# Block two's transposes by VectorE squares and DRAM, and Fourier tables as one row per product

## The chip, the cores and the metric

The kernel runs on one core of one Trainium2 chip. The metric is the device time of one execution in microseconds (us). Engines are named as the profile names them: PE is TensorE (PEld its weight loads), DVE is VectorE, ACT is ScalarE, POOL is GpSimd, SP is SyncE, which issues most DMAs.

## The reference

Three stages run one after the other on 4 batches of 768 tokens with 320 features.

- Attention: a recurrence over 768 steps with a 40 x 40 state for each of 4 batches and 8 heads.
- Block one: the real part of a two-dimensional Fourier transform (over tokens and over features) is added to x; the sum u is normalised over features, and `u + relu(un @ w_ch1) @ w_ch2` is the result (320 to 1280 to 320).
- Block two: `u = x + (relu(xt @ w_tok1) @ w_tok2)` over tokens (768 to 256 to 768), and then `u + relu(u @ w_ch1) @ w_ch2` over features (320 to 1536 to 320).

## The kernel before

Every operation of the program is first written into a plan (class `Plan`, L64) with its engine, an estimated cost, what it reads and writes, and a stage name. `emit` (L104) then simulates the engines and writes the instructions in the order in which the simulation starts them. Of the operations that are ready on an engine it takes the one with the smallest latest start, which is the length of the path behind it times a factor, plus an offset for each stage from the table `OFF` (L637). So one program order per engine comes out, and the engines keep to it. While the simulation sees PE with nothing to do it may put in small matmuls on an identity matrix (`warm`, L50), which compute nothing that is used.

Numbers are kept in two parts, a high one and a low one, each of a type that PE multiplies at its fast rate; a product is high x high, high x low and low x high, summed in PSUM.

Block one, for each batch b:

- `fft(b)` (L828) folds the tokens and the features, splits the result into `Xh` and `Xl`, and multiplies with the table `T1`, separately for even and odd frequencies (`par`). For each of 4 blocks of features, 3 chunks k of tokens and 2 parities it issues three matmuls into columns of one PSUM tile `psA` of 386 columns: Xh with the table's high part, Xh with its low part, Xl with its high part (L860). Three tiles (m = 0, 1, 2) hold both parities. Then ACT copies each parity of each tile into the high part `A` (L867) and DVE writes PSUM minus that into the low part (L868, L869).
- `fft2(b)` (L874) multiplies `A` with the table `T2` over features (`mix`), adds the result to X and takes the statistics.
- `norm` (L903) writes the normalised rows `un`; `turn` (L919) transposes three tiles of 128 tokens by 320 features on PE (nine 128 x 128 transposes into three PSUM tiles `trp`), ACT copies each into the high part `th`, DVE subtracts for the low part `tl` (L927 to L929). A turn serves one half (384 tokens) of a batch.
- `ch(b, half)` (L932) is the pair of products: for each of 10 columns of weights (12 in block two) one `hps` group of 8 matmuls with 384 columns (L953), ACT relu to `hh`, DVE to `hl` (L955, L956), and one `acc` group of 9 matmuls with 320 columns (L943).

Block two runs `tok(b)` (L1004, matmuls `tps`), `tok2(b)` (L1021, matmuls `t2ps`, whose results DVE adds to X), then `twice` (L911), which duplicates the last 64 features into `un`, then `turn` and `ch`. The order in which the plan is written is turn, turn, tok of the next batch, ch of half 0, tok2 of the next batch, ch of half 1; the planner moves them. The first half's output `ou` is written to DRAM by SP when its `ch` is done.

In the background, until 620 us, the weights of `ch` and of block two are decoded from their 64-bit form (`job`, L807: four DVE operations, one of ACT, two of POOL, written to DRAM by SP), and POOL's queue loads them back.

The last step of attention and `fft(0)` use the attention's PSUM banks: `fft(0)` takes three of bank group 'c' (`PA`, L1064). In later batches `fft` takes three of group 'ps', which has three buffers.

Of the kernel before, what the change touches and what calls it, by code (L numbers as in the profile page):

```python
# [636 lines left out]
OFF={'chain': 300.8, 'dec2': 5758.7, 'decay': -751.1, 'decode': 395.0, 'fft': -5021.4, 'fft2': -6464.4, 'inv': -1932.1, 'kbts': 226.7, 'kg': -6093.6,  # L637
     'load': -7697.1, 'load2': -587.1, 'load3': 1109.2, 'loada': 4793.9, 'merge': 1886.3, 'mlp': -1698.4, 'out_tile': 4045.5, 'outp': -1277.8,
     'pad': -9598.4, 'pts': -229.1, 'tok': -12470.6, 'tok2': -645.7, 'wdec': -467.6, ('chain', 0): -4282.3, ('chain', 1): -2552.8,
     ('chain', 10): 45.9, ('chain', 11): -8803.9, ('chain', 2): -3582.8, ('chain', 3): 7517.1, ('chain', 4): -1342.6, ('chain', 5): 1812.8,  # L640
     ('chain', 6): -2540.2, ('chain', 7): -577.2, ('chain', 8): 1284.2, ('chain', 9): -4815.7, ('dec2', 0): 2647.0, ('decay', 0): 1051.3,
     ('decay', 1): -1211.8, ('decay', 10): 2428.7, ('decay', 11): 6696.4, ('decay', 2): 7776.8, ('decay', 3): 2789.5, ('decay', 4): 838.9,
     ('decay', 5): -5123.2, ('decay', 6): -648.2, ('decay', 7): -4184.7, ('decay', 8): -115.8, ('decay', 9): 739.3, ('decode', 0): 4394.9,
     ('fft', 0): 1400.8, ('fft', 1): -1517.7, ('fft', 2): 5142.9, ('fft', 3): -772.4, ('fft2', 0): -5713.8, ('fft2', 1): 3968.9, ('fft2', 2): -531.5,
     ('fft2', 3): 3324.0, ('inv', 0): -6627.6, ('inv', 1): -5380.2, ('inv', 2): -2561.0, ('inv', 3): -2007.0, ('inv', 4): -7054.0, ('inv', 5): 772.7,
     ('kbts', 0): 1581.6, ('kbts', 1): 449.0, ('kbts', 10): 7708.3, ('kbts', 11): 4043.7, ('kbts', 2): -1443.5, ('kbts', 3): -321.0,
     ('kbts', 4): 5122.3, ('kbts', 5): -4668.8, ('kbts', 6): 2466.5, ('kbts', 7): -6673.4, ('kbts', 8): -3755.9, ('kbts', 9): -6836.2,
     ('kg', 0): -308.8, ('kg', 1): 2831.3, ('kg', 10): -5700.1, ('kg', 11): -4561.7, ('kg', 2): 1180.2, ('kg', 3): -2794.7, ('kg', 4): -1608.2,
     ('kg', 5): 2804.0, ('kg', 6): 3809.8, ('kg', 7): 991.9, ('kg', 8): -2008.2, ('kg', 9): 473.4, ('load', 0): 487.0, ('load', 1): -244.0,
     ('load', 10): 7910.1, ('load', 11): -2865.2, ('load', 2): -5618.2, ('load', 3): 6666.7, ('load', 4): -4962.2, ('load', 5): -6389.3,  # L650
     ('load', 6): -8728.7, ('load', 7): 2517.8, ('load', 8): -1405.1, ('load', 9): -4750.5, ('load2', 0): -4261.4, ('load2', 1): -2916.3,
# [4 lines left out]
     ('loada', 10): 2332.4, ('loada', 11): 1588.0, ('loada', 2): 15487.7, ('loada', 3): 344.7, ('loada', 4): -5744.5, ('loada', 5): 8816.6,  # L656
     ('loada', 6): 1439.9, ('loada', 7): -398.8, ('loada', 8): -3423.9, ('loada', 9): 7911.3, ('merge', 0): -6399.2, ('merge', 1): 4559.0,
     ('merge', 10): -10316.3, ('merge', 11): 790.3, ('merge', 2): 4278.3, ('merge', 3): 8872.4, ('merge', 4): -4569.1, ('merge', 5): 3968.6,
     ('merge', 6): 3218.1, ('merge', 7): 9397.1, ('merge', 8): -1894.3, ('merge', 9): 5033.2, ('mlp', 0): 6893.6, ('mlp', 1): 1432.8,
     ('mlp', 2): 2520.1, ('mlp', 3): 2527.4, ('out_tile', None): 7714.2, ('outp', 0): 1563.4, ('outp', 1): -4676.1, ('outp', 10): -1619.6,  # L660
     ('outp', 11): 896.2, ('outp', 2): -3595.4, ('outp', 3): 2664.9, ('outp', 4): 3205.8, ('outp', 5): 3534.9, ('outp', 6): 1010.5,
     ('outp', 7): -6340.7, ('outp', 8): 3125.1, ('outp', 9): 6287.3, ('pad', 0): -609.1, ('pts', 0): 3845.3, ('pts', 1): -329.9, ('pts', 10): 2473.5,
     ('pts', 11): 3044.7, ('pts', 2): 3317.6, ('pts', 3): -5427.0, ('pts', 4): -2906.4, ('pts', 5): -795.8, ('pts', 6): 4682.1, ('pts', 7): 1469.9,
# [49 lines left out]
class Mlp:  # L713


    def __init__(s,tc,at,M1,T2d,w,out,dr,NB=4):
# [111 lines left out]
    def fft(s,b):  # L828
# [7 lines left out]
        for par in range(2):
# [15 lines left out]
            c0,cn=(0,194) if par==0 else (194,192)  # L852
            for m,blocks in enumerate((((0,0),),((128,2),),((256,0),(384,2)))):
                for k0,k1 in G:
                    rk=[(v,o,x) for o in ((0,),(128,),(256,417,320,481))[m] for v in ('Xh','Xl') for x in (0,2) if k0<=x<k1]
                    def f(m=m,blocks=blocks,c0=c0,cn=cn,k0=k0,k1=k1):
                        ps=pst(hs[m])
# [3 lines left out]
                    s.pe((.33,.33,.66)[m]*(k1-k0),f,rk+[('T1',k) for k in range(k0,k1)],[('psA',hs[m][0],par),('psb',hs[m][0])]+[('A',a) for a in ((0,1),(2,3),(4,))[m]],alloc=hs[m][0] if par==0 and k0==0 else None,cols=(582,582,1164)[m]*(k1-k0))  # L861
        for m in range(3):
            ka=[('A',a) for a in ((0,1),(2,3),(4,4))[m]]
            for par,(c0,cn) in enumerate(((0,193),(194,192))):
                kp=('psA',hs[m][0],par)
                ev=lambda a,r=slice(0,128),par=par: t["A"][a][r,par:385:2]
                s.act(cn,lambda m=m,c0=c0,cn=cn,ev=ev: nc.scalar.activation(out=ev(2*m),in_=pst(hs[m])[:,c0:c0+cn],func=AF.Copy),[kp,'mid'],[ka[0]],free=[hs[m][0]])  # L867
                if m<2: f=lambda m=m,c0=c0,cn=cn,ev=ev: nc.vector.tensor_tensor(out=ev(2*m+1),in0=pst(hs[m])[:,c0:c0+cn],in1=ev(2*m).bitcast(F32),op=ALU.subtract)  # L868
                else: f=lambda m=m,c0=c0,cn=cn,ev=ev: nc.vector.tensor_tensor(out=ev(4,slice(64,128)),in0=pst(hs[m])[64:,c0:c0+cn],in1=ev(4,slice(64,128)).bitcast(F32),op=ALU.subtract)  # L869
                s.dve(.27,f,[kp,ka[0]],[ka[1]],free=[hs[m][0]])  # L870
# [254 lines left out]
```

## Time and profile before

| | |
|---|---|
| median of 3 runs | 1012.12 us (1011.55 to 1014.07) |
| the profiled execution, its time | 1013.38 us |
| the profiled execution, its span | 1011.3 us, mean granted clock 0.968 |
| PE busy | 954.5 us (94%) |
| PE weight loads busy | 910.6 us (90%) |
| DVE busy | 618.9 us (61%) |
| ACT busy | 440.2 us (44%) |
| POOL busy | 276.4 us (27%) |

The span counts from the first to the last instruction of the profile; the execution's own time is 2.1 us more. Matmuls are pipelined: the time between the starts of two matmuls is what one costs, and it is shorter than the duration that its row shows.

### The profile page before, as it was taken

Reading aid. Unit: us, or ns where it says so; the run is one execution under the profiler, and the core shown is the slowest. Engines: PE = TensorE matmul, PEld = TensorE weight load, DVE = VectorE, ACT = ScalarE, POOL = GpSimd, SP = SyncE. Lnnn points to the kernel's source line nnn. Section 1 sums busy time; section 2 is a strip of 40 time slices with the busy share of each in tenths; the row PEclk is TensorE's granted clock in tenths of the full one; section 3 lists DMA queues with packets and bytes.
Section 4 is the critical chain, followed back from the end, with each engine's and each line's share of the span. In section 5 each row is a group of like instructions: output and inputs, shape, how many; then the busy total and the mean of one; then the engine's idle time right before and its main releaser. Section 6 shows DMA issues by size and latency. Waiting matters only on the chain.

```text
span 1011.3 us, 23650 instructions
## 1 busy us (share of the span) xinstructions
PE 954.5 (94%) x9707; PEld 910.6 (90%) x9707; DVE 618.9 (61%) x1359; ACT 440.2 (44%) x910; POOL 276.4 (27%) x372
## 2 busy tenths in 40 slices
PE   7559999999999998899999999999999999999998
PEld 6548788888888888889999999999999999999998
DVE  8799397978959248998688866325242332323232
ACT  5266778789787663424322341223222222121221
POOL 8133544454653514233444434000000000000000
PEclk9787999999999879999999999999999999999999
DMA  9996878899885967254545446700000000000000
GB/s 212 199 190 129 186 178 177 190 199 216 193 196 150 270 159 278 66 179 135 171 160 162 145 145 219 292 1 1 2 20 1 20 21 1 20 20 1 20 20 21
DMA packets 140719, 125.47 MB, mean 124 GB/s; under 512 B 100867, under 2 KB 118275, under 8 KB 140483
## 3 DMA queue, kind: packets, MB, share of 16 engines
q1 hardware_dynamic: 135811, 100.29, 39.7%
q0 software_dynamic: 4800, 23.67, 6.8%
q8 instruction: 76, 1.25, 0.5%
q14 instruction: 32, 0.26, 0.1%
HBM read 85.40 MB, written 33.75 MB: 118 GB/s over the span
## 4 chain that ended last, share of the span: by engine, by line
PE 54%; DVE 4%; DMA 0%; issue 0%; ACT 0%; DVEq 0%
PE hps L953 23%; PE acc L943 22%; PE t2ps L1030 2%; PE tps L1017 2%; PE mix L887 2%; PE trp L924 1%; PE psA L860 1%; DVE un L908 0%; DVE mdt L820 0%; DVE Xl L848 0%; DVE mda L817 0%; DMA mdraw<-in_moe_w_ch_dram 0%; DVE un L909 0%; DVE A L868 0%; DVE hl L956 0%
## 5 line engine op out<-in xcount | busy, mean ns | idle before, releaser
L956 DVE SCALAR_TENSOR_TENSOR hl<-hps,hh 128x384 fp32r<-128x384 f32 x176 | 98.0, 557 | 250.6 <-ACT hh L955 250.1
L955 ACT ACTIVATE hh<-hps 128x384 fp32r<-128x384 f32 x176 | 86.3, 491 | 339.9 <-PE hps L953 338.8
L953 PE MATMUL hps<-th,v 128*128 128x384 f32 x576 | 142.4, 337 | 0.0
L943 PE MATMUL acc<-v,hh 128*128 128x320 f32 x576 | 129.1, 311 | 0.0
L953 PE MATMUL hps<-th,W 128*128 128x384 f32 x480 | 120.3, 339 | 2.6 <-DVE hl L956 2.6
L943 PE MATMUL acc<-W,hh 128*128 128x320 f32 x480 | 108.5, 312 | 0.0
L953 PEld LDWEIGHTS hps<-th,v 128*128 128x128 f32 x576 | 103.7, 188 | 0.0
L943 PEld LDWEIGHTS acc<-v,hh 128*128 128x128 f32 x576 | 97.5, 188 | 0.0
L953 PEld LDWEIGHTS hps<-th,W 128*128 128x128 f32 x480 | 86.8, 188 | 3.2 <-DVE hl L956 3.0
L943 PE MATMUL acc<-v,hl 128*128 128x320 f32 x288 | 89.0, 309 | 0.0
L821 POOL TENSOR_TENSOR mda<-mda,mdh 128x320 f32<-128x320 f32 (+2 forms) x44 | 46.8, 1063 | 131.1 <-DVE mdt L819 53.7
L943 PEld LDWEIGHTS acc<-W,hh 128*128 128x128 f32 x480 | 82.3, 190 | 0.0
L329 POOL TENSOR_SCALAR_AFFINE_SELECT RT<-RT 64x384 f32<-64x384 f32 x72 | 56.3, 804 | 78.6 <-ACT RT L238 74.9
L943 PE MATMUL acc<-W,hl 128*128 128x320 f32 x240 | 74.6, 311 | 0.0
L319 PE MATMUL kg<-am,bt 120*128 120x192 f32 x242 | 53.1, 364 | 18.3 <-ACT am L238 16.0
L953 PE MATMUL hps<-tl,v 128*128 128x384 f32 x192 | 64.6, 337 | 0.0
L319 PEld LDWEIGHTS kg<-am,bt 120*128 120x128 f32 x242 | 42.9, 207 | 22.3 <-ACT am L238 16.8
L519 POOL TENSOR_SCALAR_AFFINE_SELECT sc<-sc 64x384 f32<-64x384 f32 (+1 forms) x72 | 40.8, 567 | 72.2 <-ACT sc L238 69.7
L509 PE MATMUL sc<-rm,VZd 120*128 120x192 f32 x264 | 56.7, 349 | 3.1 <-DMA VZd<-in_vR_dram 2.0
L52 PE MATMUL warm<-ident 128*128 128x128 f32 x332 | 51.5, 304 | 5.1 <-DVE A L868 3.1
L943 PEld LDWEIGHTS acc<-v,hl 128*128 128x128 f32 x288 | 54.1, 188 | 0.0
L953 PE MATMUL hps<-tl,W 128*128 128x384 f32 x160 | 53.9, 337 | 0.0
(171 smaller groups left out, 2046.8 us busy)
## 6 DMA issues: line engine op xcount, KB each, us to landing
bt<-in_bkR_dram SPq DMA_DIRECT2D x12, 660.0 KB
mdraw<-in_moe_w_ch_dram SPq DMA_DIRECT2D x22, 320.0 KB
wS<-in_wR_dram SPq DMA_DIRECT2D x12, 335.2 KB
a<-in_aR_dram SPq DMA_DIRECT2D x12, 335.2 KB
RT<-a SPq DMA_DIRECT2D x36, 111.7 KB
LT<-in_vT_dram SPq DMA_DIRECT2D x12, 330.0 KB
VZt<-in_vT_dram SPq DMA_DIRECT2D x12, 330.0 KB
VZd<-in_vR_dram SPq DMA_DIRECT2D x12, 330.0 KB
```

The lines of the kernel that those rows point to most:

```text
L52: for x in range(m): nc.tensor.matmul(t[:,128*(x%4):128*(x%4)+128],lhsT=ident,rhs=ident,start=True,stop=True)
L319: nc.tensor.matmul(ps[:,192*x:192*x+192],lhsT=bt[:,g+x].rearrange("p v t -> p (v t)"),rhs=am[:,:,g+x],start=True,stop=True)
L329: nc.gpsimd.affine_select(out=kv,in_=kv,pattern=[[0,3*m],[1,L]],compare_op=ALU.is_gt,fill=0.0,base=0,channel_multiplier=-1)
L509: for x,g in enumerate(gs): nc.tensor.matmul(ps[:,192*x:192*x+192],lhsT=VZd[:,g].rearrange("p v t -> p (v t)"),rhs=s.rm[:,:,g],start=True, ...
L519: nc.gpsimd.affine_select(out=o,in_=o,pattern=[[0,3*m],[1,L]],compare_op=ALU.is_gt,fill=0.0,base=0,channel_multiplier=-1)
L821: P.op('POOL',.07+d*.00237,lambda: nc.gpsimd.tensor_tensor(out=g("da").bitcast(F32),in0=g("da").bitcast(F32),in1=g("dh").bitcast(F32),op=A ...
L887: nc.tensor.matmul(s.pst(h)[:,:320],lhsT=aa[:K,sl],rhs=T2[:K,tb],start=n==0,stop=n==7)
L943: nc.tensor.matmul(s.pst(acc[x]),lhsT=a[:,sl],rhs=t[w2][w][:,m],start=(m==0 and n==0),stop=(m==MT-1 and n==2))
L953: for n,(l,r) in enumerate(ops): nc.tensor.matmul(ps,lhsT=l,rhs=r,start=n==0,stop=n==7)
L955: s.act(384,lambda: nc.scalar.activation(out=t["hh"][z],in_=s.pst(h),func=AF.Relu),[kp],[('hh',z)],free=[h[0]])
L956: s.dve(.47,lambda: nc.vector.scalar_tensor_tensor(out=t["hl"][z],in0=s.pst(h),scalar=0.0,in1=t["hh"][z].bitcast(F32),op0=ALU.max,op1=ALU. ...
L1017: nc.tensor.matmul(s.pst(h),lhsT=t["k1"][x][:,k,ms],rhs=t[a][:,k],start=k==0 and n==0,stop=k==5 and n==2)
```

## The change

Four edits.

1. Six of block two's eight turns (both halves of batches 1, 2 and 3, `DT=((),(1,2,3))`) leave PE. In `turnd` DVE transposes 32 x 32 squares of X into `uA` (three instructions for each tile of 128 tokens), four DMAs on SP's queue write `uA` to a DRAM buffer `Td`, one DMA reads it back into the tile `Z` with features on partitions, and ACT and DVE make `th` and `tl` from `Z` in place of PSUM. `twice` falls away for these batches.
2. In `fft` the table is laid out so that the high and the low part of one product lie side by side. One matmul of 388 (or 384) columns, Xh with both parts, replaces two of 194 (192); the matmul of Xl with the high part stays. High x low comes out in columns of its own.
3. Each parity now has its own three PSUM tiles of 388 columns, so six tiles are taken from the same three banks. The evacuation of one parity is planned behind that parity's matmuls and has one more DVE operation for each tile, which adds the second half of the columns to `A`'s low part.
4. `OFF` has other values for the stages of the two blocks (fft, fft2, mlp, tok, tok2, pad, decode, dec2). Those of attention stay.

```diff
+    T1=np.concatenate([T1[:,2*p:2*p+2,c:c+n].reshape(384,-1) for p in range(2) for c,n in ((0,194),(194,192))],1).reshape(384,4,386)
...
+        s.Td=[dr.tile([4,32,4,288],F32,name=f"dr_T{j}") for j in range(2)]
...
-            s.mk(p,[128,3,384],"th",F32R,2); s.mk(p,[128,2,384],"tl",F32R,2); s.mk(p,[128,384],"un",F32,3)
+            s.mk(p,[128,3,384],"th",F32R,2); s.mk(p,[128,2,384],"tl",F32R,2); s.mk(p,[128,1152],"uA"); s.t["un"]=[s.t["uA"][:,384*x:384*x+384] for x in range(3)]
...
-        if b==0: hs=[at.psum(PA[m],[128,386],f"psA{m}") for m in range(3)]; pst=at.pst
-        else: hs=[s.psum('ps',[128,386],f"psA{i}") for i in range(3)]; pst=s.pst
+        if b==0: hs=[[at.psum(PA[p][m],[128,388],f"psA{m}{p}") for m in range(3)] for p in range(2)]; pst=at.pst
+        else: hs=[[s.psum('ps',[128,388],f"psA{m}{p}") for m in range(3)] for p in range(2)]; pst=s.pst
...
-                        seq=[y for o,tb in blocks for k in range(k0,k1) for y in (("Xh",o,tb,k),("Xh",o,tb+1,k),("Xl",o,tb,k))]
-                        for n,(xx,o,tb,k) in enumerate(seq):
-                            nc.tensor.matmul(ps[:,c0:c0+cn],lhsT=t[xx][:,k,o:o+128],rhs=s.at.T1[:,k,tb,c0:c0+cn],start=n==0 and k0==0,stop=n==len(seq)-1 and k1==3)
+                                nc.tensor.matmul(ps[:,:2*cn],lhsT=t["Xh"][:,k,o:o+128],rhs=T(k,tb,par,2*cn),start=n==1 and k0==0,stop=False)
+                                nc.tensor.matmul(ps[:,:cn],lhsT=t["Xl"][:,k,o:o+128],rhs=T(k,tb,par,cn),start=False,stop=n==w and k1==3)
...
+                f=lambda m=m,h=h,cn=cn,ev=ev,r=r,al=al: nc.vector.tensor_tensor(out=ev(al,r),in0=pst(h)[r,:cn],in1=ev(2*m,r).bitcast(F32),op=ALU.subtract)
+                s.dve(.27,f,[kp,ka[0]],[ka[1]],free=[h[0]])
+                f=lambda m=m,h=h,cn=cn,ev=ev,r=r,al=al,par=par: nc.vector.tensor_tensor(out=ev(al,r),in0=pst(h)[r,194-2*par:194-2*par+cn],in1=ev(al,r).bitcast(F32),op=ALU.add)
+                s.dve(.27,f,[kp],[ka[1]],free=[h[0]])
...
+    def turnd(s,b,half):
+        nc=s.nc; t=s.t; j=s.nt%2; s.nt+=1; V=nc.vector
+        Y=lambda: t["uA"].rearrange("p (q k a c) -> p q k a c",q=4,k=3,a=3)
+        for ii in range(3):
+            i=3*half+ii; xk=[('x',i,b)]; x=lambda i=i: s.at.X[:,i,b]
+            s.dve(.45,lambda x=x,ii=ii: V.transpose(Y()[:,:,0:2,ii].rearrange("p q k c -> p k q c"),x()[:,:256].rearrange("p (k q c) -> p k q c",k=2,q=4)),xk,[('Y',ii,0)]+[('un',y,z) for y in range(3) for z in range(2)],port=True)
+            for z in range(2): s.dve(.21,lambda x=x,ii=ii,z=z: V.transpose(Y()[:,2*z:2*z+2,2,ii],x()[:,256:320].rearrange("p (q c) -> p q c",c=32)),xk+[('un',ii,0)],[('Y',ii,1+z)],port=True)
+        yk=[('Y',y,z) for y in range(3) for z in range(3)]
+        for q in range(4):
+            s.P.op('SP',.81,lambda q=q: nc.sync.dma_start(out=s.Td[j][q].rearrange("p i x -> i p x"),in_=t["uA"][:,288*q:288*q+288]),yk+[('un',y,z) for y in range(3) for z in range(2)],[('Td',j,q)],data=1.62,lag=1.3)
+        s.P.op('SP',.81,lambda: nc.sync.dma_start(out=t["Z"].rearrange("p i x -> p (i x)"),in_=s.Td[j].rearrange("q p i x -> (q p) (i x)")),[('Td',j,q) for q in range(4)],['Z'],data=1.6,lag=1.3)
+        zk=['Z']
+        Z=lambda k,r=slice(0,128): t["Z"][r].rearrange("p i (k a c) -> p k a i c",k=3,a=3)[:,k]
+        w=lambda v: v.rearrange("p (a i c) -> p a i c",a=3,i=4)
+        for k in range(3):
+            th=lambda k=k: w(t["th"][j][:,k])
+            s.act(384,lambda k=k,th=th: nc.scalar.activation(out=th(),in_=Z(k),func=AF.Copy),zk,[('th',j,k)])
+            if k<2: s.dve(.47,lambda th=th,k=k: V.tensor_tensor(out=w(t["tl"][j][:,k]),in0=Z(k),in1=th().bitcast(F32),op=ALU.subtract),zk+[('th',j,k)],[('tl',j,k)],port=True)
+            else: s.dve(.47,lambda th=th: V.tensor_tensor(out=th()[64:],in0=Z(2,slice(64,128)),in1=th()[64:].bitcast(F32),op=ALU.subtract),zk,[('tl',j,k),('th',j,k)],port=True)
+        return j
...
-PA=('c','c','c')
+PA=(('c','c','c'),('c','c','c'))
+DT=((),(1,2,3))
```

## Rows read from the trace of the kernel before

**Rows 1.** Stretches: each engine's busy time, PE clock, DMA share.
```profile
387.90:471.40 83.50, 72.40 (x518) 70.29 (x517) 78.03 (x210) 34.28 (x100) 28.96 (x34) 0.98 0.53 171
500.00:695.00 195.00, 194.83 (x1260) 194.01 (x1260) 124.00 (x286) 55.61 (x126) 60.08 (x68) 1.00 0.45 151
695.00:1006.00 311.00, 311.00 (x1994) 310.65 (x1993) 105.90 (x245) 68.47 (x147) 0.00 (x0) 1.00 0.04 12
```

**Rows 2.** Same stretches, warm matmuls alone: PE, PEld, clock, DMA.
```profile
387.90:471.40 83.50, 9.17 (x60) 8.42 (x59) 0.98 0.53 171
```

**Rows 3.** Chain that ended last, from 880 us: start, us, what.
```profile
903.56 2.64 PE tps L1017 x18
...
929.28 2.64 PE t2ps L1030 x18
...
933.34 0.33 PE trp L924 x3
...
934.99 0.66 PE trp L924 x6
...
938.29 2.78 PE hps L953 x16
```

**Rows 4.** Who waited for whom on PE after 420 us.
```profile
PE hps L953 <- DVE hl L956: 2.6, 2, 1.9
PE mix L887 <- DVE hl L956: 1.9, 1, 1.9
```

**Rows 5.** Tile trp, by form: duration ns min/median/max, first and last start.
```profile
L924 PE MATMUL trp<-ident,un x96: 270/272/330, 417.4 to 971.6; 128*128 128x128 f32 x96
L924 PE MATMUL trp<-ident,X x48: 270/272/273, 704.6 to 971.3; 128*128 128x128 f32 x48
```

**Rows 6.** The whole chain again: Fourier products and products of block one.
```profile
544.11 1.99 PE psA L860 x18
546.10 1.34 PE acc L943 x9
547.45 1.39 PE hps L953 x8
```

**Rows 7.** Stretches, instructions on psA alone: PE, PEld, DVE, ACT, clock.
```profile
387.90:471.40 83.50, 22.64 (x192) 21.99 (x192) 5.99 (x18) 5.63 (x18) 0.98 0.53 171
500.00:695.00 195.00, 8.68 (x72) 8.51 (x72) 2.07 (x6) 1.97 (x6) 1.00 0.45 151
```

**Rows 8.** Timelines of POOL and PE: start, us, engine, line.
```profile
437.72 0.58 POOL L792 DMA_DIRECT2D W<-m11l  x1 [5.18 <-DMA m11l<-mda]
...
443.25 0.48 PE L943 MATMUL acc<-W,hh 128*128 128x320 f32 x2
```

**Rows 9.** DVE groups by form: busy us, mean ns.
```profile
L916 DVE COPY un<-X 128x64 f32<-128x64 f32 x48 | 6.9, 190 | 1.2 <-PE trp L924 0.5
...
L354 DVE TENSOR_REDUCE MT<-pr 128x32 f32<-128x512 f32 x6 | 4.0, 672 | 0.0
...
L367 DVE COPY MT<-Mt 128x256 f32<-128x256 f32 x6 | 2.2, 368 | 0.0
```

**Rows 10.** Timeline of DVE and SP at a turn and at the end.
```profile
931.96 0.49 DVE L1032 TENSOR_TENSOR X<-t2ps,X 128x320 f32<-128x320 f32 x1
...
936.47 0.56 DVE L929 TENSOR_TENSOR th<-trp,th 64x384 fp32r<-64x384 f32 x1
...
1006.84 1.53 SPq L972 DMA_DIRECT2D out_dram<-ou  x3
```

**Rows 11.** DMA issues: size, median us from issue to landing.
```profile
k<-dr_k1h POOLq DMA_DIRECT2D x2, 384.0 KB, 3.6
W<-m10l POOLq DMA_DIRECT2D x3, 640.0 KB, 9.1
```

**Rows 12.** ACT groups by form, 695 to 1006 us: busy, mean ns, idle before.
```profile
L927 ACT ACTIVATE th<-trp 128x384 fp32r<-128x384 f32 x24 | 10.9, 489 | 14.3 <-PE trp L924 14.3
```

More of the change, by code (lines that the diff above doesn't have):

```diff
@@ L636 @@
 RING=288
[L637 removed]
+OFF={'chain': 300.8, 'dec2': 8814.4, 'decay': -751.1, 'decode': 3119.3, 'fft': -14511.4, 'fft2': -6130.1, 'inv': -1932.1, 'kbts': 226.7, 'kg': -6093.6,
      'load': -7697.1, 'load2': -587.1, 'load3': 1109.2, 'loada': 4793.9, 'merge': 1886.3, 'mlp': -1698.4, 'out_tile': 4045.5, 'outp': -1277.8,
[L639 removed]
+     'pad': -5691.9, 'pts': -229.1, 'tok': -3279.4, 'tok2': -758.7, 'wdec': -467.6, ('chain', 0): -4282.3, ('chain', 1): -2552.8,
@@ L644 @@
[L644 to L647, printed above, removed]
@@ L656 @@
[L656 to L659, printed above, removed]
@@ L660 @@
[L660 to L663, printed above, removed]
@@ L851, in fft @@
                     s.dve(.06+n*w*.0007,lambda o=o,i=i,n=n,K=K: nc.vector.tensor_copy(out=t["Xl"][:,K,o:o+n],in_=t["Xl"][:,K,i:i+n].bitcast(F32)),kk('Xl',i),kk('Xl',o),port=True)
[L852 removed]
+            cn=(194,192)[par]
             for m,blocks in enumerate((((0,0),),((128,2),),((256,0),(384,2)))):
+                h=hs[par][m]
                 for k0,k1 in G:
                     rk=[(v,o,x) for o in ((0,),(128,),(256,417,320,481))[m] for v in ('Xh','Xl') for x in (0,2) if k0<=x<k1]
[L856 to L861 removed]
@@ L862, in fft, with f @@
-        for m in range(3):
[L863 to L870, printed above, removed]
+                    def f(h=h,blocks=blocks,cn=cn,k0=k0,k1=k1,par=par):
+                        ps=pst(h); w=len(blocks)*(k1-k0); n=0
+                        for o,tb in blocks:
+                            for k in range(k0,k1):
+                                n+=1
+                                nc.tensor.matmul(ps[:,:2*cn],lhsT=t["Xh"][:,k,o:o+128],rhs=T(k,tb,par,2*cn),start=n==1 and k0==0,stop=False)
+                                nc.tensor.matmul(ps[:,:cn],lhsT=t["Xl"][:,k,o:o+128],rhs=T(k,tb,par,cn),start=False,stop=n==w and k1==3)
@@ new lines, in fft @@
+                    s.pe(.287*len(blocks)*(k1-k0),f,rk+[('T1',k) for k in range(k0,k1)],[('psA',h[0],par),('psb',h[0])]+[('A',a) for a in ((0,1),(2,3),(4,))[m]],alloc=h[0] if k0==0 else None,cols=582*len(blocks)*(k1-k0))
+            for m in range(3):
+                ka=[('A',a) for a in ((0,1),(2,3),(4,4))[m]]; h=hs[par][m]; cn=193-par
+                kp=('psA',h[0],par)
+                ev=lambda a,r=slice(0,128),par=par: t["A"][a][r,par:385:2]
+                s.act(cn,lambda m=m,h=h,cn=cn,ev=ev: nc.scalar.activation(out=ev(2*m),in_=pst(h)[:,:cn],func=AF.Copy),[kp,'mid'],[ka[0]],free=[h[0]])
+                r,al=(slice(0,128),2*m+1) if m<2 else (slice(64,128),4)
+                f=lambda m=m,h=h,cn=cn,ev=ev,r=r,al=al: nc.vector.tensor_tensor(out=ev(al,r),in0=pst(h)[r,:cn],in1=ev(2*m,r).bitcast(F32),op=ALU.subtract)
+                s.dve(.27,f,[kp,ka[0]],[ka[1]],free=[h[0]])
+                f=lambda m=m,h=h,cn=cn,ev=ev,r=r,al=al,par=par: nc.vector.tensor_tensor(out=ev(al,r),in0=pst(h)[r,194-2*par:194-2*par+cn],in1=ev(al,r).bitcast(F32),op=ALU.add)
+                s.dve(.27,f,[kp],[ka[1]],free=[h[0]])
@@ L917, in twice, with turn, turnp @@
         return lambda ii,k: t["un"][ii][:,:128] if k==2 else s.at.X[:,3*half+ii,b,128*k:128*k+128],lambda ii,k: [('un',ii,0),('un',ii,1)] if k==2 else [('x',3*half+ii,b)]
-    def turn(s,b,half,src):
+    def turnd(s,b,half):
[18 more added lines that the diff above has]
+        return j
+    def turn(s,b,half,blk):
+        if b in DT[blk]: return s.turnd(b,half)
+        return s.turnp(b,half,(s.norm,s.twice)[blk](b,half))
+    def turnp(s,b,half,src):
         nc=s.nc; t=s.t; j=s.nt%2; s.nt+=1; src,keys=src
@@ L1000, in f @@
             s.mk(p,[128,2,320],"kh",F32R); s.mk(p,[128,2,320],"kl",F32R)
-            s.mk(p,[128,320],"ou",F32,3)
-        s.step(f,[],[('W1',h,k) for h in range(2) for k in range(3)]+['m3'])
+            s.mk(p,[128,320],"ou",F32,3); s.mk(p,[128,4,288],"Z")
+        s.step(f,[],[('W1',h,k) for h in range(2) for k in range(3)]+['m3','Z'])
     def tok(s,b):
@@ L1044, in plan @@
         for b in range(NB):
-            ja=s.turn(b,0,s.norm(b,0)); jb=s.turn(b,1,s.norm(b,1))
+            ja=s.turn(b,0,0); jb=s.turn(b,1,0)
             if b+1<NB: go(s.fft,b+1)
@@ L1056, in plan @@
         for b in range(NB):
-            ja=s.turn(b,0,s.twice(b,0)); jb=s.turn(b,1,s.twice(b,1))
+            ja=s.turn(b,0,1); jb=s.turn(b,1,1)
             if b+1<NB: go(s.tok,b+1)
```

30 lines of the change are left out of this document (22 added, 8 removed), and 8 rows, old and new, of the table OFF.

## The prediction

> **What bounds the kernel now.** I read first the stretches with each engine's busy time [rows 1], then the chain that ended last, then the waits on PE, then single tiles. The reader is to see three regimes.
>
> From 695 us to the end PE is busy 311.0 of 311.0 us at clock 1.00, DVE 105.9, POOL not at all, and 6 of the 1994 matmuls are warm ones. The chain runs there through PE alone, group behind group, the transposes `trp` among them [rows 3]. Whatever PE no longer has to do there shortens the program, as long as no wait takes its place. From 500 to 695 it is the same with a busier DVE (124 of 195 us). From 388 to 471 it is the other way round: DVE is busy 78.0 of 83.5 us, and PE has no work of its own for 83.5 - 72.4 = 11.1 us and fills 9.2 us more with warm matmuls [rows 1, 2], so 20.3 us in all. There DVE sets the pace, together with the decoding of weights: the first `acc` group starts at 443.25, when the last part of the first half of W2, asked for at 437.72, has come [rows 8]. The waits named after 420 us are DVE's too [rows 4].
>
> **The change part by part.**
>
> *Turns on DVE.* A turn is nine transposes, 0.33 us for three and 0.66 us for six on the chain [rows 3]: 0.99 us. A single one shows 270 ns [rows 5], but they are pipelined, so the distance of 110 ns is the price. Six turns leave PE in the stretch where PE is full: 6 x 0.99 = 5.9 us. Nothing of PE's comes in their place.
>
> The Trainium skill, "VectorE: DVE Perf Modes", Rules for kernel authors, speaks against this edit: a 128 x 128 transpose is to go to TensorE if a PSUM destination will do, since (The three transpose paths) VectorE turns only 32 x 32 squares. Its figure for TensorE is 390 ns, by which 54 of them would be an estimated 21 us; the trace disagrees, with 110 ns between starts, and the sum goes by that.
>
> What comes in: nine DVE transposes a turn. No row shows one. Below I bound the large one (256 elements) by the copy of 128 x 256, 0.37 us, and the small one (64 elements) by the copy of 128 x 64, 0.19 us; above, the large one by the slow reduction of 512 elements, 0.67 us [rows 9]. I take the lower ones, which are the nearest in size and kind: 3 x (0.37 + 2 x 0.19) = 2.3 us, less the six copies of `twice`, 1.1 us. So 1.2 us of DVE a turn and 7 us in all, in a stretch where DVE has 205 idle. An `hl` that waits behind one is late by 0.4, at worst 0.7 us; a group of eight or nine matmuls lies between it and its reader (1.3 to 1.4 us, [rows 6]), so PE does not wait. ACT's three copies to `th` (0.49 us each, [rows 12]) and DVE's three subtractions stay, with another source. I cost all this at nothing; if the cover failed it is the fourth rival.
>
> Four writes and a read go on SP's queue. Behind the writes stand the outputs `ou` of the half before, and nothing that PE needs.
>
> *The latency of a turn.* Today the last X of a half is written at 932.45 and its `tl` is done at 937.03 [rows 10]; the `ch` begins at 938.29 [rows 3], 5.8 us after X. By DRAM, from the last X: squares of one tile 0.75; four issues at 0.51 (three took 1.53) 2.0; landing 2.9, at most, since the last issue ends at 1008.37 and the span at 1011.3 [rows 10]; issue of the read 0.5; its landing 2.9 to 9.1, taken as 4.0, near the 3.6 us of 384 KB in a quieter stretch [rows 11] (Z is 576 KB); three copies and a subtraction 2.0. Sum 12.2 us (11.1 to 17.3). So the sums of X must be ready 12 us ahead of their `ch` in place of 6. The data allow it: the `tps` on which they rest are done at 906.2, 23 us before `t2ps` begins [rows 3], and the plan charges the new chain 0.81 + 4 x 1.62 + 1.3 + 0.81 + 1.6 + 1.3 = 12 us, so it should put `t2ps` earlier. I cost it at nothing. Half 1 has the whole of half 0 as cover.
>
> *Table rows.* 18 matmuls took 1.99 us [rows 6], three of them 0.332. Their distance is 0.111, whereas 384 columns take 1.39 / 8 = 0.174 and 320 take 1.34 / 9 = 0.149, or 0.4 ns a column: 192 columns alone would be near 0.094, so something other than columns sets it, as the same 0.110 of the transposes' 128 columns says. A matmul of 388 columns costs 0.176, that of 194 stays at 0.111: 0.287, a gain of 0.045 for each three, 24 of them (72 matmuls, [rows 7]), 1.1 us a batch. Bounds: nothing, if the wide one hides no more than before, or 0.06 (the narrow one at 0.094), 1.5 us. Batch 3 lies where PE is full, batch 2's end before it where PE is nearly full; 0 and 1 lie where PE waits anyhow. I count two: 2.2 us (1.1 to 4.4).
>
> *Evacuation.* Each batch gets six more DVE additions of 5.99 / 18 = 0.33 us [rows 7]: 2.0 us. Batch 3's lie where DVE is free a third of the time. Those of batches 0 to 2, 18 of them, 6.0 us, lie in the stretch that DVE bounds. In `fft(0)` the second parity must also wait for the first one's banks, but the first one's evacuation can begin sooner, and the matmuls are 16 x 0.045 = 0.7 us shorter. DVE's other work there (folds for batch 2, decodings) can partly slip behind 471, where DVE is less busy. So the price lies between 0 and 6.0; I take half, 3.0 us.
>
> *Offsets.* They move work between these stretches and add none. No row says which way; ±3 us at the start of block one, where 20.3 us of PE's time are at stake.
>
> **Sum** against the profiled execution: 1013.38 (span 1011.3 and 2.1 around it) - 5.9 - 2.2 + 3.0 = 1008.3. The median of the runs shown is 1.26 lower, so 1007.0 for a median.
>
> **The rivals.**
>
> 1. *The start gives nothing up.* The additions fit beside other work and the new order uses some of PE's 20.3 us: -5.9 - 2.2 - 2 gives 1002. For it: the decodings have until 620 us. Against: DVE is 93% busy there. Chance 0.20.
> 2. *The start takes it back.* All 6.0 us of additions are on the path and only batch 3's tables count: -5.9 - 1.1 + 6.0 gives 1011, no change. Chance 0.15.
> 3. *Slower: PE waits for the trip through DRAM.* If `t2ps` stays where it is, each of three batches begins 12.2 - 5.8 = 6.4 us late, 19 us in all: 1007.0 + 19 = 1026. It decides once a batch loses more than (5.1 + 3.0) / 3 = 2.7 us, that is when the last X of half 0 stands less than 9.5 us ahead of its `ch`. For it: one order, written by a simulation, with a latency that this trace can't confirm. Against: the 23 us of room. Chance 0.09.
> 4. *The rule of the page holds another way:* each of 18 large squares holds `hl` up and PE with it, at up to 0.67 us: 12.1 us, which gives 1019. Against: DVE's 34% and the margin of a whole group. (The page is the one named above.) Chance 0.03.
>
> **How the numbers follow.** The forecast, 1007.0 with a range of its own from 1003 to 1010.5, has 0.53. What a measurement can tell from no change is about 0.3%, 3.0 us: faster means under 1009.1, slower over 1015.2. Faster: 0.47 of the forecast's 0.53, and rival 1's 0.20, together 0.67. Same: the rest of the forecast, 0.06, and 0.12 of rival 2: 0.18. Slower: rivals 3 and 4, and 0.03 of rival 2 if the offsets add to it: 0.15. The range reaches below to the whole gain of the tables with the offsets' 3 us (-5.9 - 4.4 - 2.5, 999.5), above to rival 2 with some of them, 1013.5; rivals 3 and 4 stay outside.
>
> **What would show it.** In the changed kernel's profile: no `trp` from the second batch of block two on, and PE still full from its first `tps` to the end, with that stretch shorter by 5.9 us; no wait of PE on ACT's `th` or DVE's `tl` ahead of a batch (rival 3), none on `hl` (rival 4); pairs of `psA` matmuls 0.29 us apart; the first `acc` group near 443 to 446, and PE's idle and warm time up to there a little over 20 us (rival 2: 25 or more). Wrong it would be if the first `tps` of block two came later by more than 3 us, or if PE idled where a batch of block two begins.

## The result, and the profile after

The changed kernel takes 1001.51 us (median of 17 runs), the kernel before 1014.68 us beside it: ratio 0.9878, 95% interval 0.9854 to 0.9901, so 12.4 us faster by the ratio. In a second set of runs (run 6) the ratio was 0.9913 (0.9881 to 0.9944), 8.8 us. The forecast was 5.1 us. The profiled execution after took 999.66 us, with a span of 998.0. Ratios are of undisturbed executions alone; the profiled ones of runs 8 and 9 below were slow (mean granted clocks 0.959 and 0.961), so their stretches are read together with their ratios.

First the stretches, cut at three marks: the last `X` of attention, the first `acc` group, the first `tps` of block two, the end. Columns: stretch, length, then busy time (and instructions) of PE, PEld, DVE, ACT, POOL, then PE's clock, DMA share and GB/s. The kernel before:

```profile
388.50:443.30 54.80, 45.60 (x335) 43.79 (x335) 51.04 (x136) 21.16 (x62) 19.09 (x22) 0.97 0.54 180
443.30:695.00 251.70, 249.62 (x1611) 248.47 (x1610) 167.82 (x397) 76.69 (x181) 80.41 (x90) 0.99 0.45 150
695.00:1011.30 316.30, 312.16 (x2000) 311.54 (x1998) 107.27 (x248) 68.47 (x147) 0.00 (x0) 1.00 0.04 13
```

The kernel after:

```profile
386.80:437.10 50.30, 43.91 (x280) 41.62 (x279) 47.20 (x136) 20.48 (x58) 16.91 (x21) 0.93 0.59 196
437.10:688.30 251.20, 249.91 (x1592) 247.70 (x1592) 179.41 (x421) 77.10 (x185) 80.28 (x92) 1.00 0.46 151
688.30:998.00 309.70, 306.30 (x1946) 305.95 (x1944) 113.58 (x266) 68.01 (x147) 0.00 (x0) 1.00 0.11 36
```

Block two is 6.6 us shorter: PE has exactly 54 instructions and 5.86 us less to do, and 0.74 us went from the tail behind the last matmul. In block one the 4.5 us were gained ahead of the first `acc`, where DVE is still 94% busy; behind it, where PE is full, nothing changed. Attention's end came 1.7 us earlier, which lies within what it varies by anyhow (last section).

PE's timeline in batch 1's Fourier products, after: pairs, 0.29 us from start to start of each pair, as forecast; in [rows 6] three matmuls took 0.332.

```profile
401.94 0.36 PE L866 MATMUL psA<-T,Xh 128*128 128x388 f32 x1
402.15 0.25 PE L867 MATMUL psA<-T,Xl 128*128 128x194 f32 x1
402.24 0.36 PE L866 MATMUL psA<-T,Xh 128*128 128x388 f32 x1
402.44 0.25 PE L867 MATMUL psA<-T,Xl 128*128 128x194 f32 x1
402.53 0.36 PE L866 MATMUL psA<-T,Xh 128*128 128x388 f32 x1
```

Tiles `uA` and `trp`, after (duration ns min/median/max, first and last start). The 18 + 36 transposes on DVE take 0.446 and 0.202 us, for which 0.37 and 0.19 were taken; the last `trp` on PE is at 736.7, against 971 in [rows 5].

```profile
L934 DVE STREAM_TRANSPOSE uA<-X x36: 200/202/246, 744.4 to 938.8; 128x64 f32<-128x64 f32 x36
L933 DVE STREAM_TRANSPOSE uA<-X x18: 401/446/449, 744.0 to 938.4; 128x256 f32<-128x256 f32 x18
...
L957 PE MATMUL trp<-ident,uA x78: 270/272/329, 422.9 to 736.7; 128*128 128x128 f32 x78
L957 PE MATMUL trp<-ident,X x12: 270/272/273, 699.6 to 736.4; 128*128 128x128 f32 x12
```

The trip through DRAM, first turn of batch 1, on SP's and ACT's timeline; then ACT's wait summed over block two (total us, times, longest):

```profile
765.34 2.42 SPq L937 DMA_DIRECT2D dr_T<-uA  x4
774.14 0.33 SPq L938 DMA_DIRECT2D Z<-dr_T  x1
...
778.33 1.35 ACT L944 ACTIVATE th<-Z 128x384 fp32r<-128x384 f32 x3 [6.80 <-DMA Z<-dr_T]
```

```profile
ACT th L944 <- DMA Z<-dr_T: 8.8, 4, 6.8
```

The four writes are issued by 767.76 and the read only at 774.14: 6.4 us of landing, where at most 2.9 was taken. From the last X (764.70) to `tl` (780.51) the trip takes 15.8 us, not 12.2, though inside the bound of 17.3. In the waits of block two PE has none, before or after.

### The profile page after: what moved, and what is told of

Its sections match the earlier page's. It is cut to its first block, busy times and chain, and to the rows that moved or that the text cites. A ratio compares the mean times of both kernels' runs of the same rounds, so it can differ in the third digit from the quotient of the medians.

```text
span 998.0 us, 23467 instructions
## 1 busy us (share of the span) xinstructions
PE 940.2 (94%) x9571; PEld 893.7 (90%) x9571; DVE 632.2 (63%) x1401; ACT 439.2 (44%) x910; POOL 271.0 (27%) x372
## 4 chain that ended last, share of the span: by engine, by line
PE 52%; DVE 6%; DMA 1%; issue 1%; ACT 0%; SPq 0%; DVEq 0%; ACTq 0%
PE hps L986 22%; PE acc L976 21%; PE t2ps L1063 2%; PE tps L1050 2%; PE mix L896 2%; DMA mdraw<-in_moe_w_tok_dram 1%; PE psA L866 1%; PE trp L957 1%; DVE mda L820 1%; PE warm L52 1%; PE psA L867 0%; DVE F L845 0%; DVE hl L989 0%; DVE Xl L852 0%; DVE A L875 0%
## 5 line engine op out<-in xcount | busy, mean ns | idle before, releaser
L824 POOL TENSOR_TENSOR mda<-mda,mdh 128x320 f32<-128x320 f32 (+2 forms) x44 | 44.7, 1016 | 122.3 <-ACT mdh L821 62.8
L329 POOL TENSOR_SCALAR_AFFINE_SELECT RT<-RT 64x384 f32<-64x384 f32 x72 | 53.5, 767 | 82.1 <-ACT RT L238 78.4
L319 PEld LDWEIGHTS kg<-am,bt 120*128 120x128 f32 x242 | 40.3, 198 | 26.3 <-ACT am L238 18.9
```

Source lines behind the costliest of these rows:

```text
L319: nc.tensor.matmul(ps[:,192*x:192*x+192],lhsT=bt[:,g+x].rearrange("p v t -> p (v t)"),rhs=am[:,:,g+x],start=True,stop=True)
L329: nc.gpsimd.affine_select(out=kv,in_=kv,pattern=[[0,3*m],[1,L]],compare_op=ALU.is_gt,fill=0.0,base=0,channel_multiplier=-1)
L824: P.op('POOL',.07+d*.00237,lambda: nc.gpsimd.tensor_tensor(out=g("da").bitcast(F32),in0=g("da").bitcast(F32),in1=g("dh").bitcast(F32),op=A ...
```

## The experiments

Each run was timed against the kernel before on its own chip. Because attention's end moves by several us from execution to execution, the parts are read from the lengths of the stretches: block one from attention's last `X` to the first `tps`, block two from there to the end. Each length is one reading, of one profiled execution; five readings of block one with the same order and tables spread over 3.0 us (table below). The first theories were: A, the gain at the start comes from the new order; B, from the new tables and their evacuation; C, from attention or chance.

**1 to 4: one part at a time** (one chip).

The new order alone, in the kernel before:

```diff
-OFF={... 'fft': -5021.4, ...
+OFF={... 'fft': -14511.4, ...
```

> The kernel before with nothing but the new offsets, so the same operations in another order. Theory A (the unforecast 5 to 7 us at the start of block one come from the new order: W2's decoding goes ahead of the folds for batch 2): about 6 us faster than before (ratio near 0.994), the first acc group near 437 to 439 us of the profile in place of 443.25. Theory B (they come from the Fourier edit itself: each parity's own tiles let the evacuation begin sooner): no change, ratio 0.998 to 1.003. Theory C (attention's last stretch or chance made the profiled run short): no change either, and e2 and e3 show no share of it.

Ratio 0.9997 (0.9963 to 1.0032); block one 303.9 us, block two 316.6. The first `acc` came at 436.8, as theory A had it, but the stretch behind it grew by 6.7 us, so the place of that mark alone is no measure of the gain.

The changed kernel with the order of the kernel before (the reverse edit of `OFF`):

> The changed kernel with the old offsets. Theory A: the turns' 6 to 6.6 us and about nothing at the start, ratio near 0.994. Theory B: as the changed kernel, ratio near 0.988. Theory of the forecast (a price of 3 us at the start that the new order then wins back): ratio near 0.995. If the old offsets leave t2ps late, PE waits at each batch for the trip through DRAM, and it is slower by up to 19 us.

Ratio 0.9974 (0.9941 to 1.0007); block one 310.2, block two 309.6.

The changed kernel with all turns on PE:

```diff
-DT=((),(1,2,3))
+DT=((),())
```

> The changed kernel with all turns of block two on PE again (new offsets, new Fourier tables). Both theories A and B: the turns' 5.9 to 6.6 us come back and the start keeps its gain, ratio to before near 0.994. Theory C (the start's gain is chance): ratio near 1.000.

Ratio 0.9991 (0.9956 to 1.0026); block one 301.4, block two 316.8. By its time this is what theory C expected (the start's gain is chance); by the stretches block one kept its gain of 5 us, as A and B expected.

The turns on DVE alone: `fft`, the table, `PA` and `OFF` of the kernel before.

```diff
-PA=(('c','c','c'),('c','c','c'))
+PA=('c','c','c')
```

> The kernel before with the six turns by DVE and DRAM alone (old offsets, old Fourier tables). If the turns are worth what the stretch of full PE says, 5.9 to 6.6 us: ratio near 0.994. If PE waits for the trip through DRAM (15.8 us from the last X to tl in the changed kernel's trace, where 5.8 us of cover stood before): slower by up to 19 us, ratio 1.01 or more, with waits on th or tl ahead of a batch.

Ratio 0.9961 (0.9929 to 0.9992); block one 306.9, block two 309.6.

Block two is shorter by 6.6 to 6.7 us wherever the turns are on DVE and not at all elsewhere, so that part stands by itself. In block one neither A nor B holds alone: the new order gives 2.6 us with the old tables, the new tables cost 3.5 with the old order, both together give 5.0. These are differences of single readings, and the times do not show them as well: runs 1 and 3, which by their blocks should be 2.3 and 4.6 us faster than the kernel before, are 0.3 and 0.9 faster. So that block one is shorter is shown by the stretches of many runs, but how much of it reaches the whole time is less sure.

**5: turns and the new order, old tables** (the same edit of `fft`, the table and `PA`, with the new `OFF`), a second reading of that cell.

> The changed kernel with the tables and the evacuation of the kernel before: turns on DVE and the new order alone. Sum theory (each part has its own price): block one as with the new order alone, 303 to 304.5 us, block two 309.6, together 9 us under before, ratio 0.991. Rival (the new order is worth something only with the new tables, and the 303.9 of the run with the new order alone was chance): block one 306 to 307, ratio 0.9935.

Ratio 0.9906 (0.9872 to 0.994); block one 305.3, block two 309.6. The ratio is that of the sum; the stretch lies between the two theories.

**6: the changed kernel again.**

> The changed kernel once more, unchanged, on the chip of the runs beside it. Blocks theory (attention's end varies from execution to execution by several us, and what the change does stands in the blocks alone): block one again 301 to 302 us from attention's last X to block two's first tps and block two again 309.7; attention's end anywhere from 386 to 398; ratio to the kernel before 0.988 (0.985 to 0.991). Chip theory (part of the 12 us was the first chip's): the ratio comes out at 0.992 or more, with the blocks' lengths as before.

Ratio 0.9913 (0.9881 to 0.9944); block one 303.4, block two 309.6, attention's end 389.7. Block one lies above the 301 to 302 expected. The ratio lies between the two expectations, and the intervals of both sets meet, so the chip theory is neither shown nor excluded; the chip of the first set isn't on record. That attention's end varies is shown: five programs with the same order up to block two have it at 385.8, 386.8, 389.7, 393.0 and 402.5 us.

**7 and 8: what the additions cost.** Both leave out the 24 additions of the second columns, so the products of X's high part with the table's low part are missing from the spectrum; every other instruction and the order stay. One run has the new order, one the old.

```diff
-f=lambda ...: nc.vector.tensor_tensor(out=ev(al,r),in0=pst(h)[r,194-2*par:...],in1=ev(al,r).bitcast(F32),op=ALU.add)
+f=lambda: None
```

> The changed kernel without the 24 additions of the table's second half in the evacuation (so the products of X's high part with the tables' low part are left out of the spectrum), all else and the order kept. New-order theory (under the new order the additions lie beside other work): block one 300 to 302 us, as with them (301.5), time within 0.2%. Rival (they cost half, as forecast, and the order gained 8 us elsewhere): block one 298 to 299, 3 us faster.

> The same leaving out of the 24 additions, in the changed kernel with the order of the kernel before (with them: block one 310.2 us, first acc 449.0, the kernel 1014.4). Additions theory (under the old order all 18 additions of batches 0 to 2, 6.3 us, are on DVE's path): block one 303.5 to 305, 6 us faster. Rival (the old order itself is bad for the new tables, for instance since the folds' matmuls of one parity now wait for other banks, and the additions are a small part): block one 308 to 310, at most 2 us faster.

New order: 0.9845 (0.9808 to 0.9883) against 0.9913 of run 6 on the same chip, 0.68% or 6.9 us, with intervals that just meet; block one 296.4, 4.7 to 7.7 under the five readings with additions. Old order: 0.9918 (0.9889 to 0.9948) against 0.9974 on another chip, 5.7 us; block one 303.9, 6.3 less than 310.2. So the additions theory holds, and the new-order theory (they lie beside other work) fell; its rival's 298 to 299 was passed too. The rows without additions, first the new order up to the first `acc`, then the old one up to it and behind it:

```profile
392.50:439.00 46.50, 40.35 (x279) 38.51 (x279) 44.32 (x124) 20.30 (x58) 16.87 (x20) 1.00 0.62 207
```

```profile
401.10:453.10 52.00, 45.07 (x286) 43.38 (x286) 47.42 (x126) 20.94 (x60) 19.00 (x22) 0.90 0.57 189
453.10:705.00 251.90, 250.14 (x1594) 248.37 (x1594) 173.27 (x408) 76.02 (x183) 80.69 (x90) 1.00 0.46 150
```

The same two stretches of the old order with the additions (run 2):

```profile
394.50:449.00 54.50, 45.51 (x285) 42.96 (x284) 50.77 (x137) 21.29 (x60) 19.34 (x22) 0.91 0.55 178
449.00:704.70 255.70, 251.12 (x1596) 248.32 (x1595) 177.07 (x420) 75.93 (x183) 80.85 (x90) 1.00 0.46 148
```

Under the old order the two runs have nearly the same clock (0.90 and 0.91), so its difference is the cleaner one: twelve additions each way, 4.1 us of DVE in either stretch, give 2.5 us ahead of the first `acc`, where DVE is 93% busy, and 3.8 behind it, where DVE is 69% busy on average. Behind it the first 29 us are alike in both runs, with PE full, and the loss comes after them: PE idles 4.6 us there with the additions and 1.8 without, mostly in waits on DVE's results. Under the new order the clock differs and takes a share. In five runs with that order DVE's work up to the first `acc` is the same, and the stretch is longer the lower PE's mean granted clock (49.6, 49.7, 50.3, 51.6 and 52.4 us at 0.97, 0.97, 0.93, 0.90 and 0.88); a mean below 1.00 says that the clock was at the lower of its two levels (1.2 GHz) for a part of the stretch. The shortest and the longest (runs 3 and 12):

```profile
393.00:442.60 49.60, 42.89 (x281) 40.56 (x280) 47.12 (x136) 20.39 (x58) 16.90 (x21) 0.97 0.58 192
402.50:454.90 52.40, 47.00 (x283) 44.86 (x282) 47.18 (x136) 20.69 (x58) 16.87 (x21) 0.88 0.55 181
```

Run 7 had 1.00 there. So under the new order the 4.7 to 7.7 us hold both the additions and the clock, and no run parts the two.

**9 and 10: which half of the order.** The changed kernel with the old offsets for the decoding of weights alone (`dec2`, `decode`, `pad`), and with the old ones for the folds and the block's other stages (`fft`, `fft2`, `mlp`, `tok`, `tok2`).

```diff
-'dec2': 8814.4, ... 'decode': 3119.3, ... 'pad': -5691.9
+'dec2': 5758.7, ... 'decode': 395.0, ... 'pad': -9598.4
```

> The changed kernel with the old offsets for the decoding of weights alone (dec2, decode, pad); the folds, fft2, mlp and tok keep the new ones. Fold theory (the new order gains because batch 2's folds are put behind the first products): block one 301 to 303.5, as with all the new offsets (301.1 to 303.4), block two 309.7. Decoding theory (it gains because W2's decoding comes ahead): first acc 3 us or more later from attention's last X, block one 307 to 310.

> The other half: the changed kernel with the old offsets for the folds, fft2, mlp and tok, and the new ones for the decoding of weights. Fold theory: block one 308.5 to 311, as with all the old offsets (310.2). Decoding theory: block one 301 to 304.

Old decoding: 0.9872 (0.983 to 0.9913), block one 304.6, first `acc` 50.4 us behind attention's last X, as with all the new offsets. Old folds: 0.9968 (0.9934 to 1.0001) on the same chip, block one 308.8, first `acc` after 56.0. So the values for folds, `fft2`, `mlp` and `tok` carry most of the order's gain; 304.6 lies 1.1 us above the range of the fold theory, so a small share of the decoding isn't excluded. The reason that the theory gave isn't shown by this: with the new tables both orders have the same number of fold operations ahead of the first `acc` (below).

All readings of block one together, last `X` to first `acc` + first `acc` to first `tps`, us:

| order | old tables | new tables | new tables without additions |
|---|---|---|---|
| old | 54.8 + 251.7 = 306.5; 57.0 + 249.9 = 306.9 | 54.5 + 255.7 = 310.2; 56.0 + 252.8 = 308.8 (decoding new) | 52.0 + 251.9 = 303.9 |
| new | 45.5 + 258.4 = 303.9; 46.3 + 259.0 = 305.3 | five runs, 301.1 to 304.1, mean 302.3; 50.4 + 254.2 = 304.6 (decoding old) | 46.5 + 249.9 = 296.4 |

**11: a longer trip** (order of every engine kept).

(`f` lays a buffer out as 128 rows.)

```diff
+nc.sync.dma_start(out=f(s.Tx[j]),in_=f(s.Td[j]))
-nc.sync.dma_start(out=t["Z"]...,in_=f(s.Td[j]))
+nc.sync.dma_start(out=t["Z"]...,in_=f(s.Tx[j]))
```

> The trip of a turn through DRAM made longer by one more hop (DRAM to DRAM, ahead of the read), the order of every engine kept. Room theory (the trip is hidden by the room that the order leaves ahead of each batch): the hop costs 4 to 7 us; the first batch of block two that takes the trip has 2.4 us of room (tl ends 780.5, its ch begins 782.9), so PE waits there 2 to 5 us, in one place; the second one has 16 us of room and waits for nothing. Block two 312 to 315 us, ratio to the unchanged changed kernel 1.002 to 1.005. Rival (the room is equal at all three, or the trip isn't on any path): three waits, 6 to 15 us; or none at all and the same time.

Ratio 1.0046 (1.002 to 1.0073) against 0.9913 of run 6 on the same chip: 13.5 us lost, block two 326.3 in place of 309.6. The room theory fell; the loss is nearer to its rival's 6 to 15 us, though not by three waits ahead of a batch: the hop takes 4.3 us (issues at 772.70 and 776.97), and six trips lose 16.7 us. ACT's timeline in this run at the second turn of batch 1:

```profile
802.28 1.35 ACT L948 ACTIVATE th<-Z 128x384 fp32r<-128x384 f32 x3 [5.60 <-DMA Z<-dr_Tx]
803.54 0.85 ACT L992 ACTIVATE hh<-hps 128x384 fp32r<-128x384 f32 x2
```

PE's timeline at the same place:

```profile
804.06 0.56 PE L980 MATMUL acc<-v,hh 128*128 128x320 f32 x2 [2.47 <-ACT hh L992]
805.09 0.41 PE L980 MATMUL acc<-v,hl 128*128 128x320 f32 x1 [0.47 <-DVE hl L993]
```

PE's waits in the whole of block two (total us, times, longest):

```profile
PE hps L990 <- DVE hl L993: 5.9, 4, 1.9
PE acc L980 <- ACT hh L992: 3.0, 2, 2.5
PE acc L980 <- DVE hl L993: 0.9, 2, 0.5
```

The reader is to see that it isn't the next `ch` that is late: none of these waits is for `th` or `tl`. ACT takes its queue in order, `th` stands in it ahead of the `hh` of the `ch` that is running, and while ACT waits 5.6 us for Z, PE runs out of `hh` and waits 2.47 + 0.47 us. What counts here is where `th` stands on ACT, not how far off its reader on PE is. The waits add up to 9.8 us. The rest of the 16.7 goes with a longer busy time of PE, 312.7 us for 306.3, at a mean granted clock of 0.99 for 1.00; from 800 to 812 us, where the waits shown are, the clock was 0.86 in the mean. How much the clock took isn't parted. The unchanged trip's 6.8 us of waiting fell into a hole of ACT.

**12: a shorter trip** (order kept): the 128 partitions as the outer dimension of each write in DRAM, the read as four.

```diff
-dr.tile([4,32,4,288],...)
+dr.tile([4,4,32,288],...)
-dma_start(out=s.Td[j][q].rearrange("p i x -> i p x"),in_=t["uA"][:,288*q:288*q+288])
+dma_start(out=s.Td[j][q].rearrange("a b x -> (a b) x"),in_=t["uA"][:,288*q:288*q+288])
...
+for q in range(4): nc.sync.dma_start(out=t["Z"][32*q:32*q+32],in_=s.Td[j][q].rearrange("i p x -> p i x"))
```

> A turn's four writes laid out so that the 128 partitions are the outer dimension in DRAM, not the four groups, and the read as four transfers of 32 partitions; the order of every engine kept. Engines theory (the writes are slow because only some of the 16 DMA engines take part, 0.27 of them): the time from the last write's issue to the issue of the read falls from 6.5 us to 2.5 to 4, and ACT waits for Z 3 to 4 us less. The time stays where it is, within 0.2% of the unchanged changed kernel, since PE waits for nothing there. Rival (a write to DRAM and its semaphore take this long however it is cut): still 6 us or more. Second rival (ACT's wait for Z, 8.8 us in all, costs PE something that the waits don't show): 2 us or more faster in block two.

Ratio 0.9895 (0.9848 to 0.9943), block two 310.0: the time stays. The trip itself, first turn of batch 1, on SP's and ACT's timeline:

```profile
783.60 1.79 SPq L937 DMA_DIRECT2D dr_T<-uA  x4
785.49 1.85 SPq L939 DMA_DIRECT2D Z<-dr_T  x4
...
790.29 1.35 ACT L946 ACTIVATE th<-Z 128x384 fp32r<-128x384 f32 x3 [0.48 <-DMA Z<-dr_T]
```

From the first write's issue to `th` it takes 6.7 us, not 13.0; ACT waits 0.5 us in block two, not 8.8. The rival (6 us or more however it is cut) fell. The gain is larger than the engines theory put it, but not all of it is the writes': each of the four reads can start behind its own write, where the one read waited for all four (the first read is issued 0.1 us behind the last write's issue, not 6.4), and the run doesn't part the two. The second rival falls: the trip is off the path in the changed kernel, as forecast.

## Why the prediction came out as it did

- **Turns: right, in mechanism and size.** 5.86 us of PE against 5.9. Nothing took their place: no wait of PE on `th`, `tl` or `hl` in block two (rivals 3 and 4 didn't come). The rule that was weighed (the Trainium skill, "VectorE: DVE Perf Modes", Rules for kernel authors: a 128 x 128 transpose to TensorE if PSUM will do) did not hold in this case, where TensorE is the bounding engine: 54 transposes cost PE 5.9 us, while DVE's 54 take 15.3 us (18 x 0.446 + 36 x 0.202) in a stretch where it has 196 free.
- **The latency of a turn: the sum was mis-sized, the conclusion right, its reason too wide.** The landing of the writes is 6.4 us, not 2.9. The 23 us of room between `tps` and `t2ps` aren't the room: run 11 shows that 4.3 us more already cost 16.7. Rival 3's threshold, 9.5 us from X to `ch`, was wrong as a mechanism; the trip counts from ACT's place for `th`, and there the order has less than 4.3 us to spare.
- **Table rows: right.** 0.29 us a pair. Without the additions the new tables shorten block one by 2.8 us under the old order (306.7, the mean of two, to 303.9, a single reading); 2.2 was counted, with a bound of 4.4. That they give 8.2 under the new order (304.6 to 296.4) is more than that bound: less PE work alone doesn't explain it. The earlier start of each parity's evacuation, the way the order fits and the clock (1.00 up to the first `acc` in run 7, 0.94 and 0.96 in the old tables' runs) may each have a part; no run parts these.
- **Evacuation: mis-sized.** Half of the 6.0 us was taken. Run 8 shows 6.3 at a like clock, and run 7 4.7 to 7.7 with the clock in it: about all of the 6.0, as rival 2 had it. The place was wrong as well: only the stretch that DVE bounds, to 471 us, was to pay, but 3.8 of the 6.3 us lie behind it, in waits of PE on DVE where PE is otherwise full.
- **Offsets: the step that failed.** They "move work between these stretches and add none", 0 with 3 either way. With the new tables they are worth 7.2 us (309.5 to 302.3, means of the cells above; 5.7, 309.5 to 303.8, against the two readings of the new order with a like clock, runs 6 and 12), with the old ones 2.1 (306.7 to 304.6), which is less than readings of one cell spread by. The sign that the prediction named, a first `acc` near 443 to 446, did not come: it was 437.1.

By means the sum is -6.6 (turns) - 2.8 (tables) + 5.6 (additions) - 7.2 (order) = -11.0 us, between the 12.4 and 8.8 of the two sets. That the parts add up to the difference of the blocks follows from how they are taken, so it is no further test of each. The time came out at rival 1's number (1002), and its place, the start, is right; its reason is half right: the start does pay for the additions, and the order gives back more than that. So that the time lay within the stated range is in part luck: the additions cost 2.6 us more than was counted, and the order, counted at nothing, gave back more than twice that. (The lower end of the range is also mis-added: with the 3 us for the offsets it is 998.8, not 999.5.) The times of runs 1 to 4 lie 0.4 to 3.7 us above what their blocks alone would give, the last (run 3) at the edge of its interval; that stays open.

What the order does: in the three runs shown next DVE is 93 to 94% busy in the stretch to the first `acc` (over all runs 86 to 95%). DVE's groups there (busy us, mean ns | idle before), first the kernel before, then the kernel after, then the changed kernel in the old order:

```profile
L848 DVE TENSOR_TENSOR Xl<-ef,Xh 128x384 fp32r<-128x384 f32 (+5 forms) x16 | 7.8, 508 | 0.0
...
L841 DVE TENSOR_TENSOR F<-X 128x960 f32<-128x960 f32 x4 | 4.6, 1142 | 0.0
```

```profile
L877 DVE TENSOR_TENSOR A<-psA,A 128x193 fp32r<-128x193 f32 (+3 forms) x12 | 4.0, 352 | 0.2
L852 DVE TENSOR_TENSOR Xl<-ef,Xh 128x384 fp32r<-128x384 f32 (+5 forms) x12 | 3.8, 345 | 0.0
...
L845 DVE TENSOR_TENSOR F<-X 128x960 f32<-128x960 f32 x3 | 3.4, 1138 | 0.0
...
L823 DVE SCALAR_TENSOR_TENSOR mdt<-mdraw,mdt 128x320 f32<-128x320 uint16 x6 | 3.0, 501 | 0.0
```

```profile
L822 DVE SCALAR_TENSOR_TENSOR mdt<-mdraw,mdt 128x320 f32<-128x320 uint16 x7 | 6.0, 853 | 0.0
L851 DVE TENSOR_TENSOR Xl<-ef,Xh 128x384 fp32r<-128x384 f32 (+5 forms) x12 | 5.3, 452 | 0.0
```

Against the kernel before, the 4.0 us of additions came in (L877), and fewer folds stand there (F three times for four, Xl 12 times for 16 and 4.0 us less). Against the old order with the same tables, nearly the same operations (137 in the old order, 136 in the new) take 47.2 us and not 50.8, since several are shorter, `mdt` 501 ns for 853. The old order also has PE waiting, ahead of the first `acc` for `uA` and behind it for `hl`, as the waits of that run in block one show (total us, times, longest); the new order has no wait for `uA`, and 0.5 us for `hl` at a `trp`:

```profile
PE trp L956 <- DVE uA L916: 4.5, 4, 1.7
...
PE trp L956 <- DVE hl L988: 2.9, 2, 2.1
```

That the shorter operations come from fewer meetings with POOL (below) is argued from the rows; no run tested it.

## What to carry to other kernels

A part that is off the bounding engine is priced by leaving it out in either order, not by halving its busy time: here 8.2 us of additions on DVE cost about 6, and more of it where DVE is 69% busy on average than where it is 93% busy. An order tuned together with an edit isn't a neutral term: it can be worth more than the edit, and most of it only with that edit. A transfer's room is counted from the first in-order queue that waits for it, and from what stands behind the waiting instruction there.

## What the runs showed of the hardware

**Writes with four outer rows use a quarter of the DMA engines.** Stretches while the four writes land, first the kernel after, then run 12, where all of the second stretch lies ahead of the first read's issue (785.49):

```profile
768.00:770.00 2.00, 2.00 (x14) 2.00 (x13) 0.01 (x1) 0.35 (x1) 0.00 (x0) 1.00 0.27 88
770.00:772.00 2.00, 2.00 (x14) 2.00 (x13) 1.00 (x2) 0.63 (x2) 0.00 (x0) 1.00 0.27 93
```

```profile
783.60:785.60 2.00, 2.00 (x15) 2.00 (x14) 0.10 (x1) 0.40 (x1) 0.00 (x0) 1.00 0.50 176
784.50:785.50 1.00, 1.00 (x8) 1.00 (x7) 0.00 (x0) 0.30 (x1) 0.00 (x0) 1.00 0.85 298
```

The DMA share is 0.27 at some 90 GB/s with an outer dimension of 4, and 0.85 at 298 GB/s with 128. Run 12 also moved the rows in DRAM next to each other, and no run parts that from the number of engines; for the engines speaks the share itself, near a quarter. The Trainium skill, "DMA: Bandwidth & Descriptors", Why a DMA increments its semaphore by 16 and not by 1, says that a DMA uses the largest number of engines up to 16 that divides the slowest dimension of both sides; for 4 rows that is a quarter of them, and the trace agrees.

**A DVE copy can wait while POOL works.** A copy of 128 x 64 takes 0.19 us [rows 9]; in the kernel before one that starts at 429.56 takes 2.10, to 431.66, while POOL issues a DMA and runs two additions without a gap from 429.30 to 431.60. DVE's timeline, then POOL's:

```profile
429.56 2.10 DVE L909 COPY un<-un 128x64 f32<-128x64 f32 x1
```

```profile
429.30 0.58 POOL L792 DMA_DIRECT2D W<-m11h  x1 [0.76 <-DVE un L909]
429.89 0.89 POOL L822 TENSOR_TENSOR mda<-mda,mdt 128x320 fp32r<-128x320 f32 x1
430.73 0.87 POOL L821 TENSOR_TENSOR mda<-mda,mdh 128x320 f32<-128x320 f32 x1
```

The Trainium skill, "SBUF — State Buffer", SBUF: two separate sides, says that VectorE and GpSimd share a pair of ports by an exclusive lock, which the instruction that starts first holds for its whole length, and that copies are among the VectorE instructions that can take it; these rows agree, with the copy ending only when POOL's run of work does.

**Attention varies by up to 16.7 us.** The same order ends it between 385.8 and 402.5 us, over several chips; the two readings known to be of one chip are 385.8 and 389.7. With the latest end went the lowest mean clock of the five, 0.963 against 0.970 to 0.974. One profile's span therefore can't be compared with another's to a few us; its stretches can.
